# A linear-attention and MLP kernel: batch 2 loaded through POOL's queue, g spread by a DMA, and the first columns of w_in loaded in row pieces

## The chip, the cores and the metric

The kernel runs on one core of a Trainium2 chip. The core has a matrix engine (TensorE, called PE in the profile; its weight loads are the row PEld), a vector engine (VectorE, DVE), an activation engine (ScalarE, ACT), a general engine (GpSimd, POOL) and a queue engine that only issues transfers (SyncE, SP). Each engine takes its instructions in order. Transfers are issued from SP, ACT or POOL; SP and ACT hand them to hardware queues (q1 and q10 in the profile), POOL to the software queue (q0), which can also change the type on the way (float32 in memory to float16 on the chip). Matmuls write to PSUM, which has eight banks; VectorE and ScalarE read results from there.

The metric is the device time of one execution in microseconds, the median of several runs.

## The reference

Eight batches, eight heads, 576 rows, 64 columns per head. All inputs and the output are float32.

```python
kv  = einsum('bhsd,bhse->bhde', k, v)          # per head: k^T v, 64 x 64
out = einsum('bhsd,bhde->bhse', q, kv)
rms = sqrt(mean(out * out, axis=-1) + 1e-6)
x   = out / rms * g_norm                       # per head, then heads side by side: 4608 x 512
h   = x @ w_in                                 # 512 x 2048
y   = (h * sigmoid(1.702 * h)) @ w_out         # 2048 x 512
```

## The kernel before

**Tiling.** The MLP runs in nine steps, t = 0 to 8. Step t below 8 takes 512 of the 576 rows of batch t; the last step takes the 8 x 64 rows that are left over (`x_rem`). Within a step the hidden part makes 16 columns of 128 (`fo`), each by four matmuls (`ko`, line 457) into one PSUM bank, and ScalarE applies the gate (line 466) to float16 in `gT`. Then the output part makes four blocks of 128 rows (`mo`), each by 16 matmuls (line 492), and VectorE or ScalarE copies a block from PSUM (line 502); step 0 goes over its blocks in turns of four matmuls (`deep`), its first two blocks in pool ps_h, its last two in ps_o. The output is stored from SP (line 549 for steps 0 and 1, in eight pieces).

**Attention** of batch t + 1 is woven into step t by lists of due places: `at1(i, ...)` puts a call behind column i of the hidden part, `at2(i, ...)` behind matmul i of the output part. No planner decides anything: instructions go to each engine in the order in which the program writes them.

Batches 0 and 1 are loaded by POOL's queue straight to float16, 96 rows to a partition group (`early_load`, line 90); only batch 0's first pair of heads comes by SP and ACT. Batches 2 to 7 are loaded as float32 by SP (`load_batch`, lines 109 to 128): whole tiles `kf`, `vf`, `qf` of 1 MB, and the 64 rows left over, `krf`, `vrf`, `qrf`, in rows of 256 bytes. `casts(b)` then makes float16 of them, the tiles on VectorE and the rows on POOL (lines 130 to 143), `transpose_q` transposes q by DMA from SP, `kv` makes the 64 x 64 products (lines 220 to 235, with the left-over rows in a last matmul, line 233), `rows` and `turn` make the normalised rows, and a DMA transpose brings them to `xT`.

**Batch 2's load** is issued in step 0's output part. Its first tile is first written by a one-element POOL copy that reads the last tile of batch 1 (line 115), so that SP starts it when batch 1 has landed.

**The start.** Batch 0 goes pair by pair (two heads each; class `First`): `q(c)` transposes, `kv(c)` multiplies, `out(c)` makes q times kv, ScalarE squares, `sums(c)` adds up by a matmul with ones and takes the logarithm, `rs(c)` is the exponential, and `apply(c)` on VectorE (line 353) writes row block c of `xT`. Row block c is what the four-matmul sum of every hidden column needs at ko = c. The order of all this and of the first six columns (`GROUP`) is written out by hand, lines 579 to 627, with `busy(n)`, n matmuls whose result nobody reads, in between. POOL's queue holds, in order: pairs 1 to 3 of batch 0, w_in in five pieces (lines 181 to 185), w_out in four pieces and batch 1.

**PSUM.** ps_a (tag "att") has three banks, ps_h ("hT") three, ps_o ("o") two. A tile gets a bank that was released; a bank is released when the last reader of its tile in program order is done.

**g.** `g_col` (g along partitions, for `apply`) comes from two tiny matmuls (line 590). `g_all` (g along the free dimension on all partitions, for `turn`) comes from a matmul with a row of ones and a VectorE copy (`spread_g`, lines 636 to 639), behind column 9 of step 0.

Of the kernel before, what the change touches and what calls it, by code (L numbers as in the profile page):

```python
# [16 lines left out]
def kernel(  # L17
# [60 lines left out]
    ones_r = const.tile([1, P], F32)  # L78
# [30 lines left out]
    def load_batch(b, landed=None):  # L109
        tiles = {}  # L110
        for n in "kvq":
            t = tiles[n] = stage.tile([P, H, J * D], F32, name=f"{n}f", tag=f"{n}f")
            if landed is not None and n == "k":

                nc.gpsimd.tensor_copy(t[0:1, 0, 0:1], landed)
            nc.sync.dma_start(  # L116
                out=t, in_=srcs[n][b, :, 0:SM, :].rearrange("h (p j) d -> p h (j d)", j=J)
            )
        for n in "kv":
            t = tiles[n + "r"] = stage.tile([R, H, D], F32, name=f"{n}rf", tag=f"{n}rf")  # L120
            nc.sync.dma_start(out=t, in_=srcs[n][b, :, SM:S, :].rearrange("h p d -> p h d"))
        t = tiles["qr"] = stage.tile([P, 4, D], F32, name="qrf", tag="qrf")
        for g in range(2):
            nc.sync.dma_start(
                out=t[g * R : (g + 1) * R],
                in_=q[b, 4 * g : 4 * g + 4, SM:S, :].rearrange("h p d -> p h d"),
            )
# [53 lines left out]
    load_w_in(0, 4, 0, 2)  # L181
    load_w_in(0, 4, 2, KO)
    load_w_in(4, GROUP)
    load_w_in(GROUP, 10)
    load_w_in(10, FO)
# [8 lines left out]
    nc.vector.memset(ones_r, 1.0)  # L194
# [171 lines left out]
    class First(Attention):  # L366
# [4 lines left out]
        def kv(self, c):  # L371
            t = ps_o.tile([P, D], F32, name="kv0", tag="o")
# [16 lines left out]
        def q(self, c):  # L389
            t = ps_h.tile([P, S], F16, name="q0", tag="hT")  # L390
# [77 lines left out]
    def dense(t, units1, units2, group, deep, hid=None):  # L468
        hid = hid or Hidden(t)
        gT = hid.gT  # L470
        if group and t:
            for ko in range(KO):
                for fo in range(group):
                    hid.mm(ko, fo, *((ps_h, "hT") if fo < 3 else (ps_a, "att")))
# [106 lines left out]
    busy(2)  # L581
    a0.kv(0)
    busy(2)
    a0.out(0)
    a0.q(1)
    a0.kv(1)
    g_ps = ps_o.tile([P, 1], F32, name="g_ps", tag="o")
    for hl in range(2):
        r = slice(hl * D, (hl + 1) * D)
        nc.tensor.matmul(g_ps[r, :], g_row, one_t, start=True, stop=True)  # L590
    nc.vector.tensor_copy(g_col, g_ps)
    a0.sums(0)
    a0.out(1)
    a0.q(2)
    a0.rs(0)
    busy(1)
    a0.kv(2)
    a0.sums(1)
    a0.apply(0)
    busy(1)  # L600
    a0.out(2)
    a0.rs(1)
    a0.q(3)
    a0.kv(3)
    a0.sums(2)
    a0.apply(1)
    a0.out(3)
    a0.rs(2)
    a0.apply(2)
    busy(3)  # L610
    d0 = Hidden(0)
    for fo in range(4):
        d0.mm(0, fo, *((ps_h, "hT") if fo < 3 else (ps_a, "att")))
        if fo == 2:
            a0.ss(3)
# [115 lines left out]
```

## Time and profile before

| | us |
|---|---|
| median of five runs | 290.12 |
| lowest and highest | 288.58 and 290.89 |
| the profiled execution, its time | 289.17 |
| its span, first to last instruction | 287.1 |
| PE busy in it | 280.4 |
| ACT, DVE, POOL busy | 156.4, 110.9, 43.6 |
| granted TensorE clock | 1.0 throughout |

The profile shows one execution. A row of an engine's instructions in order of time gives the start in us from the beginning of the span, the time taken, the engine, the line of the kernel, the operation, the result and operands by the program's names, the shapes, how many instructions were merged (x29), and in brackets how long the engine was idle before and what ended that. A matmul's time runs from its start to its modelled end, and the next one starts before that, so the times of a row of matmuls overlap.

### The profile page before, as it was taken

What the parts mean: (1) busy time and instruction counts of PE and PEld (TensorE: products, weight loads), DVE (VectorE), ACT (ScalarE), POOL (GpSimd) and SP (SyncE); (2) the same over time, 40 slices, a digit from 0 to 9 for tenths busy, and PEclk for the clock granted to TensorE, in tenths of its full rate; (3) what the DMA queues carried; (4) which work ended last, traced back from release to release, by engine and by line L of the source; (5) the groups of instructions that cost most, each with busy time, mean ns of one, the idle gap of its engine ahead of it and who ended that gap; (6) DMA issues with size and microseconds to landing.
All of it is one profiled execution on the core that took longest, in us unless ns stands there. A gap on an engine that the chain in (4) does not pass through costs nothing.

```text
span 287.1 us, 4102 instructions
## 1 busy us (share of the span) xinstructions
PE 280.4 (98%) x1611; PEld 136.5 (48%) x1611; DVE 110.9 (39%) x221; ACT 156.4 (54%) x273; POOL 43.6 (15%) x59
## 2 busy tenths in 40 slices
PE   7899999999999999999999999999999999999994
PEld 2444544454445544554455445544554444444443
DVE  2530534437651566148603861376227400110011
ACT  2696457856565745584467536763666365017400
POOL 8941000301300140015000510032001100000000
PEclk9999999999999999999999999999999999999999
DMA  8999999979989736892879558953601130011022
GB/s 174 204 204 205 205 203 342 221 179 355 204 174 322 171 73 202 250 270 56 184 176 346 80 164 202 345 86 110 158 0 37 37 148 0 0 73 75 0 73 73
DMA packets 67300, 45.79 MB, mean 160 GB/s; under 512 B 37714, under 2 KB 65106, under 8 KB 66514
## 3 DMA queue, kind: packets, MB, share of 16 engines
q1 hardware_dynamic: 58064, 37.28, 50.0%
q0 software_dynamic: 8496, 7.29, 15.9%
q10 hardware_dynamic: 722, 0.97, 1.2%
q8 instruction: 12, 0.20, 0.3%
q14 instruction: 6, 0.05, 0.1%
HBM read 36.70 MB, written 9.44 MB: 161 GB/s over the span
## 4 chain that ended last, share of the span: by engine, by line
PE 84%; DMA 8%; POOL 2%; DVE 2%; SPq 2%; ACT 1%; issue 0%; POOLq 0%
PE hT L457 40%; PE o L492 37%; DMA krf<-in_k_dram 3%; DMA vbuf<-in_v_dram 2%; PE kvp L225 2%; PE outR L291 2%; DMA xT<-x 1%; PE oh L522 1%; SPq L116 1%; DMA out_dram<-osb 1%; POOL qraw L90 1%; ACT gT L466 1%; DVE kbuf L138 1%; PE ss L339 1%; POOL kraw L90 1%; PE outT L259 1%
## 5 line engine op out<-in xcount | busy, mean ns | idle before, releaser
L492 PE MATMUL o<-w_out_sb,gT 128*128 128x512 f16 x560 | 130.7, 379 | 0.0
L466 ACT ACTIVATE gT<-hT 128x512 f16<-128x512 f32 x144 | 84.8, 598 | 77.6 <-PE hT L457 77.5
L457 PE MATMUL hT<-xT,w_in_sb 128*128 128x512 f16 x512 | 116.4, 379 | 0.3 <-DMA xT<-x 0.3
L457 PEld LDWEIGHTS <-w_in_sb 128*128 128x128 f16 x576 | 55.1, 98 | 62.7 <-DMA xT<-x 0.8
L492 PEld LDWEIGHTS <-gT 128*128 128x128 f16 x560 | 53.0, 98 | 56.3 <-issue 0.2
L502 DVE COPY osb<-o 128x512 f32<-128x512 f32 x20 | 13.8, 691 | 63.5 <-PE o L492 63.5
L323 POOL TENSOR_TENSOR x<-xr,g_all 128x512 f16<-128x512 f32 x12 | 15.2, 1268 | 141.6 <-DVE xr L316 119.0
L240 DVE CAST kvb<-kvp 64x256 f16<-64x256 f32 (+1 forms) x16 | 6.2, 388 | 42.7 <-PE kvp L233 41.6
L302 DVE TENSOR_REDUCE sum<-sq 128x8 f32<-128x512 f16 x24 | 15.8, 678 | 17.5 <-ACT sq L299 17.5
L316 DVE TENSOR_TENSOR xr<-outR,sum 128x512 f32<-128x512 f32 x24 | 15.5, 686 | 11.1 <-ACT sum L313 11.1
L323 DVE TENSOR_TENSOR x<-xr,g_all 128x512 f16<-128x512 f32 x12 | 15.2, 1264 | 0.7
L299 ACT ACTIVATE sq<-outR 128x512 f16<-128x512 f32 x24 | 13.6, 591 | 2.0 <-PE outR L291 1.6
L279 ACT ACTIVATE sq<-outT 128x512 f16<-128x512 f32 (+1 forms) x16 | 7.7, 482 | 11.7 <-PE outT L259 10.4
L457 PE MATMUL hT<-x_rem,w_in_sb 128*128 128x512 f16 x64 | 14.0, 379 | 0.0
L502 ACT COPY osb<-o 128x512 f32<-128x512 f32 x15 | 8.7, 580 | 6.3 <-PE o L492 6.3
L312 ACT ACTIVATE sum<-sum,eps_t 128x16 f32<-128x16 f32 x12 | 3.7, 308 | 15.0 <-DVE sum L302 14.9
L341 ACT ACTIVATE ln<-ss,eps_t 128x512 f32<-128x512 f32 (+1 forms) x16 | 9.4, 585 | 3.2 <-PE ss L339 3.1
L138 DVE CAST qbuf<-qf 128x512 f16<-128x512 f32 x24 | 9.0, 436 | 3.8 <-DMA qf<-in_q_dram 3.8
L466 ACT ACT_TABLE_LOAD x8 | 10.3, 1283 | 0.1
L225 PEld LDWEIGHTS <-kbuf 128*128 128x128 f16 x96 | 7.4, 98 | 5.7
L291 PEld LDWEIGHTS <-qTd 128*128 128x128 f16 x96 | 7.4, 98 | 5.7 <-issue 0.2
L225 PE MATMUL kvp<-vbuf,kbuf 128*128 128x128 f16 x96 | 9.3, 219 | 0.0
(71 smaller groups left out, 152.6 us busy)
## 6 DMA issues: line engine op xcount, KB each, us to landing
kf<-in_k_dram SPq DMA_DIRECT2D x6, 1024.0 KB, 5.8
vf<-in_v_dram SPq DMA_DIRECT2D x6, 1024.0 KB, 8.4
qf<-in_q_dram SPq DMA_DIRECT2D x6, 1024.0 KB, 11.0
out_dram<-osb SPq DMA_DIRECT2D x6, 1024.0 KB, 4.3
w_out_sb<-in_moe_w_out_dram POOLq DMA_DIRECT2D x4, 512.0 KB, 16.8
out_dram<-osb SPq DMA_DIRECT2D x6, 192.0 KB, 3.2
out_dram<-osb SPq DMA_DIRECT2D x7, 128.0 KB, 2.4
w_in_sb<-in_moe_w_in_dram POOLq DMA_DIRECT2D x3, 256.0 KB, 6.7
```

The costliest lines, as they stand in the source:

```text
L138: nc.vector.tensor_copy(out=dst[:, c, :, :].rearrange("p j (l d) -> p j l d", l=2), in_=src[n][:, h, :].rearrange("p l (j d) -> p j l d", ...
L225: nc.tensor.matmul(t[:, c, :].rearrange("p (l d) -> p l d", l=2), kh[:, c, j, :], vh[:, 2 * c : 2 * c + 2, j * D : (j + 1) * D], start=(j ...
L291: nc.tensor.matmul(t[:, c * P : (c + 1) * P], self.qT[c][:, j * P : (j + 1) * P], self.kb[:, c, :], start=True, stop=True,)
L299: nc.scalar.activation(sq, t, AFT.Square)
L302: nc.vector.tensor_reduce(out=self.sum2[:, j % 2, :], in_=sq.rearrange("p (h d) -> p h d", h=H), op=ALU.add, axis=mybir.AxisListType.X,)
L316: nc.vector.tensor_mul(xr[:, i], self.o[j + i].rearrange("p (h d) -> p h d", h=H), s2[:, i, :].unsqueeze(2).to_broadcast([P, H, D]),)
L323: (nc.vector if i else nc.gpsimd).tensor_mul(self.x16[:, j + i, :].rearrange("p (h d) -> p h d", h=H), xr[:, i], g_all.unsqueeze(1).to_bro ...
L341: nc.scalar.activation(ln[:, 0:n], t[:, 0:n], AFT.Ln, bias=eps_t, scale=1.0 / D)
L457: nc.tensor.matmul(self.h[fo], w_in_sb[:, ko, fo * P : (fo + 1) * P], self.x[:, ko], start=(ko == 0), stop=(ko == KO - 1),)
L466: nc.scalar.activation(self.gT[:, fo, :], self.h[fo], AFT.Gelu_apprx_sigmoid)
L492: nc.tensor.matmul(os[mo], gT[:, fo, mo * P : (mo + 1) * P], w_out_sb[:, fo, :], start=(fo == 0), stop=(fo == FO - 1),)
L502: copy(osb[:, mo, :], os[mo])
```

## The change

Six edits:

- `load_batch` takes a queue, and loads q first, then the left-over rows of q, then k, v and their rows. Batch 2 is loaded by POOL's queue, issued behind the last of w_out and batch 1; the one-element copy that made SP wait is gone. Batches 3 to 7 stay on SP, in the new order.
- `g_all` is loaded by a DMA that repeats g over 128 partitions, on POOL's queue behind batch 2; `spread_g` and its row of ones are gone.
- w_in goes in seven pieces: row block 0 of columns 0 to 3 ahead of batch 0's last pair, then row block 1, row block 2 of these columns, row blocks 0 to 2 of columns 4 and 5, row block 3 of columns 0 to 5, and columns 6 to 7, 8 to 10 and 11 to 15 whole.
- The start's order is rewritten: first matmuls on w_in stand ahead of pair 3's transposes, and all six columns get their ko = 3 matmul last. Fillers go from 21 to 19. Pair 3 uses other PSUM pools. `g_col` is made earlier.
- Step 1 begins with a group of five columns instead of four; its first eight matmuls are as before, then the fifth column's first two, and the fifth column stands in ps_o.
- In step 1, the casts of batch 2, its transposes and the load of batch 3 stand behind column 5 instead of 7, and its kv products begin behind column 10 instead of 11.

```diff
--- before.py
+++ after.py
@@ -75,7 +75,6 @@
     eps_t = const.tile([P, 1], F32)
     g_col = const.tile([P, 1], F32)
     g_all = const.tile([P, D], F32)
-    ones_r = const.tile([1, P], F32)
     w_in_sb = const.tile([P, KO, DFF], F16)
     w_out_sb = const.tile([P, FO, DM], F16)
     x_rem = const.tile([P, KO, B * R], F16)
@@ -106,25 +105,23 @@
     qh = qbuf[:, 0 : NPAIR * SM].rearrange("p (c j e) -> p c j e", c=NPAIR, j=J)
     vh = vbuf.rearrange("p c x -> p (c x)")[:, 0 : NPAIR * SM].rearrange("p (h x) -> p h x", h=H)
 
-    def load_batch(b, landed=None):
+    def load_batch(b, queue=nc.sync):
         tiles = {}
-        for n in "kvq":
+        for n in "qkv":
             t = tiles[n] = stage.tile([P, H, J * D], F32, name=f"{n}f", tag=f"{n}f")
-            if landed is not None and n == "k":
-
-                nc.gpsimd.tensor_copy(t[0:1, 0, 0:1], landed)
-            nc.sync.dma_start(
+            queue.dma_start(
                 out=t, in_=srcs[n][b, :, 0:SM, :].rearrange("h (p j) d -> p h (j d)", j=J)
             )
+            if n == "q":
+                t = tiles["qr"] = stage.tile([P, 4, D], F32, name="qrf", tag="qrf")
+                for g in range(2):
+                    queue.dma_start(
+                        out=t[g * R : (g + 1) * R],
+                        in_=q[b, 4 * g : 4 * g + 4, SM:S, :].rearrange("h p d -> p h d"),
+                    )
         for n in "kv":
             t = tiles[n + "r"] = stage.tile([R, H, D], F32, name=f"{n}rf", tag=f"{n}rf")
-            nc.sync.dma_start(out=t, in_=srcs[n][b, :, SM:S, :].rearrange("h p d -> p h d"))
-        t = tiles["qr"] = stage.tile([P, 4, D], F32, name="qrf", tag="qrf")
-        for g in range(2):
-            nc.sync.dma_start(
-                out=t[g * R : (g + 1) * R],
-                in_=q[b, 4 * g : 4 * g + 4, SM:S, :].rearrange("h p d -> p h d"),
-            )
+            queue.dma_start(out=t, in_=srcs[n][b, :, SM:S, :].rearrange("h p d -> p h d"))
         staged[b] = tiles
 
     def casts(b):
@@ -178,11 +175,15 @@
     for c in range(1, NPAIR):
         for n in "qkv"[c == 1 :]:
             early_load(n, 0, c, c + 1)
-    load_w_in(0, 4, 0, 2)
-    load_w_in(0, 4, 2, KO)
-    load_w_in(4, GROUP)
-    load_w_in(GROUP, 10)
-    load_w_in(10, FO)
+        if c == NPAIR - 2:
+            load_w_in(0, 4, 0, 1)
+    load_w_in(0, 4, 1, 2)
+    load_w_in(0, 4, 2, 3)
+    load_w_in(4, GROUP, 0, 3)
+    load_w_in(0, GROUP, 3, KO)
+    load_w_in(GROUP, 8)
+    load_w_in(8, 11)
+    load_w_in(11, FO)
 
     nc.scalar.preload_act_table_set("natural_log_exp_and_others")
     nc.vector.memset(ones2, 0.0)
@@ -191,7 +192,6 @@
     nc.vector.memset(eps_t, EPS)
     one_t = const.tile([1, 1], F32)
     nc.vector.memset(one_t, 1.0)
-    nc.vector.memset(ones_r, 1.0)
 
 
     def load_w_out(f0, f1):
@@ -369,7 +369,8 @@
         ss_pool = (ps_o, "o")
 
         def kv(self, c):
-            t = ps_o.tile([P, D], F32, name="kv0", tag="o")
+            pool, tag = (ps_o, "o") if c < NPAIR - 1 else (ps_a, "att")
+            t = pool.tile([P, D], F32, name="kv0", tag=tag)
             for j in range(NJ):
                 for hl in range(2):
                     x = slice((hl * NJ + j) * D, (hl * NJ + j + 1) * D)
@@ -387,7 +388,8 @@
             )
 
         def q(self, c):
-            t = ps_h.tile([P, S], F16, name="q0", tag="hT")
+            pool, tag = (ps_h, "hT") if c < NPAIR - 1 else (ps_o, "o")
+            t = pool.tile([P, S], F16, name="q0", tag=tag)
             for j in range(NJ):
                 for hl in range(2):
                     nc.tensor.transpose(
@@ -469,9 +471,11 @@
         hid = hid or Hidden(t)
         gT = hid.gT
         if group and t:
-            for ko in range(KO):
-                for fo in range(group):
-                    hid.mm(ko, fo, *((ps_h, "hT") if fo < 3 else (ps_a, "att")))
+            order = [(ko, fo) for part in (range(4), range(4, group)) for ko in (0, 1) for fo in part]
+            order += [(ko, fo) for ko in range(2, KO) for fo in range(group)]
+            for ko, fo in order:
+                pool = (ps_h, "hT") if fo < 3 else (ps_a, "att") if fo == 3 else (ps_o, "o")
+                hid.mm(ko, fo, *pool)
             for fo in range(group):
                 hid.gate(fo)
         for fo in range(FO):
@@ -578,51 +582,55 @@
 
     busy(12)
     a0.q(0)
-    busy(2)
     a0.kv(0)
-    busy(2)
-    a0.out(0)
-    a0.q(1)
-    a0.kv(1)
     g_ps = ps_o.tile([P, 1], F32, name="g_ps", tag="o")
     for hl in range(2):
         r = slice(hl * D, (hl + 1) * D)
         nc.tensor.matmul(g_ps[r, :], g_row, one_t, start=True, stop=True)
+    busy(2)
+    a0.out(0)
     nc.vector.tensor_copy(g_col, g_ps)
+    a0.q(1)
+    a0.kv(1)
     a0.sums(0)
     a0.out(1)
+    busy(1)
     a0.q(2)
     a0.rs(0)
+    a0.sums(1)
     busy(1)
     a0.kv(2)
-    a0.sums(1)
     a0.apply(0)
+    a0.rs(1)
+    busy(2)
+    a0.out(2)
     busy(1)
-    a0.out(2)
-    a0.rs(1)
-    a0.q(3)
-    a0.kv(3)
+    d0 = Hidden(0)
+    d0.mm(0, 0)
+    d0.mm(0, 1)
+    d0.mm(0, 2)
     a0.sums(2)
     a0.apply(1)
+    a0.q(3)
+    a0.rs(2)
+    a0.kv(3)
+    d0.mm(1, 0)
+    d0.mm(1, 1)
     a0.out(3)
-    a0.rs(2)
+    d0.mm(1, 2)
+    d0.mm(0, 3, ps_a, "att")
+    d0.mm(1, 3)
     a0.apply(2)
-    busy(3)
-    d0 = Hidden(0)
-    for fo in range(4):
-        d0.mm(0, fo, *((ps_h, "hT") if fo < 3 else (ps_a, "att")))
-        if fo == 2:
-            a0.ss(3)
-            a0.apply(3)
-    for ko in (1, 2):
-        for fo in range(4):
-            d0.mm(ko, fo)
-    for ko in range(KO - 1):
-        d0.mm(ko, 4, ps_o, "o")
-    for fo in range(GROUP - 1):
+    d0.mm(2, 0)
+    a0.ss(3)
+    a0.apply(3)
+    for fo in range(1, 4):
+        d0.mm(2, fo)
+    for fo in range(4, GROUP):
+        for ko in range(3):
+            d0.mm(ko, fo, ps_o, "o")
+    for fo in range(GROUP):
         d0.mm(KO - 1, fo)
-    for ko in range(KO):
-        d0.mm(ko, GROUP - 1, ps_o, "o")
     for fo in range(GROUP):
         d0.gate(fo)
     load_w_out(0, 4)
@@ -632,11 +640,9 @@
         early_load("k", 1, c, c + 2)
         early_load("v", 1, c, c + 2)
         load_w_out(8 + 2 * c, 12 + 2 * c)
-
-    def spread_g():
-        t = ps_a.tile([P, D], F32, name="ga_ps", tag="att")
-        nc.tensor.matmul(t, ones_r, g_row, start=True, stop=True)
-        nc.vector.tensor_copy(g_all, t)
+    load_batch(2, nc.gpsimd)
+
+    nc.gpsimd.dma_start(out=g_all, in_=g_norm.unsqueeze(0).to_broadcast([P, D]))
 
     live = {0: a0}
 
@@ -662,7 +668,6 @@
             at2(4, of(0, "ss", NPAIR, True))
             at2(4, of(0, "apply", NPAIR))
             at1(8, start, 1)
-            at1(9, spread_g)
             for r in krem + vrem:
                 at1(8, nc.vector.memset, r[R:P], 0.0)
             for c in range(NPAIR):
@@ -674,21 +679,20 @@
                 at2(o, of(1, "out", c))
                 at2(o + 7 - c // 2, of(1, "ss", c))
                 at2(o + 7 - c // 2, of(1, "apply", c))
-            at2(14, load_batch, 2, vbuf[0:1, NPAIR - 1, 0:1])
         elif b < B:
             if t == 1:
                 at2(46, setattr, live[1], "ss_pool", Attention.ss_pool)
                 at2(46, of(1, "out", NPAIR))
                 at2(53, of(1, "ss", NPAIR))
                 at2(53, of(1, "apply", NPAIR))
-            f0 = 7 if t == 1 else 2
+            f0 = 5 if t == 1 else 2
             at1(f0, casts, b)
             at1(f0, start, b)
             at1(f0, of(b, "transpose_q"))
             if t + 2 < B:
                 at1(f0, load_batch, t + 2)
             for c in range(NPAIR):
-                at1((11 if t == 1 else 9) + c, of(b, "kv", c))
+                at1((10 if t == 1 else 9) + c, of(b, "kv", c))
             at2(6, nc.scalar.preload_act_table_set, "natural_log_exp_and_others")
             for j in range(J):
                 at2((1, 4, 8, 11)[j], of(b, "rows", j))
@@ -697,7 +701,7 @@
             at2(27, of(b, "out", NPAIR))
             at2(36, of(b, "ss", NPAIR))
             at2(36, of(b, "apply", NPAIR))
-        dense(t, u1, u2, (GROUP, 4)[t] if t < 2 else 0, t == 0, None if t else d0)
+        dense(t, u1, u2, (GROUP, 5)[t] if t < 2 else 0, t == 0, None if t else d0)
 
 
 # ---- launch: one core; inputs and outputs as the reference has them ----
```

## The prediction

> **What bounds the kernel now.** I read the page first, then the chain in order of time, then each engine's instructions in order of time for 5 to 20 us and 38 to 80 us.
>
> ```profile
> PE 280.4 (98%) x1611; PEld 136.5 (48%) x1611; DVE 110.9 (39%) x221; ACT 156.4 (54%) x273; POOL 43.6 (15%) x59
> ```
>
> TensorE is the bound. A busy matmul is drawn 379 ns long, but the next starts 216 ns after it (24 of them between 23.95 and 28.92 us: 4.97 / 23), so "busy" hides small waits, and I look for them in start-to-start distances. After 13 us all excess over the usual distances comes to only 1.9 us. That caps what better order can bring there; the rest must come from the first 14 us, where filler matmuls run.
>
> ```profile
> 12.89 0.38 PE L376 MATMUL kv<-vbuf,kraw 96*64 96x64 f16 x12 [0.58 <-DMA vbuf<-in_v_dram]
> 13.20 0.39 PE L339 MATMUL ss<-sq,ones 128*128 128x512 f16 x1
> 13.66 0.39 PE L259 MATMUL outT<-qT,kvb 128*128 128x512 f16 x1
> 13.88 0.81 PE L571 MATMUL idle<-kvb 128*128 128x512 f16 x3
> 14.53 0.81 PE L457 MATMUL hT<-xT,w_in_sb 128*128 128x512 f16 x3
> 15.18 0.38 PE L339 MATMUL ss<-sq,ones 128*128 128x512 f16 x1
> 15.39 6.42 PE L457 MATMUL hT<-xT,w_in_sb 128*128 128x512 f16 x29
> ```
>
> Here the last pair's values land at 12.76, the first matmul on w_in starts at 14.53, and from 15.39 on there is no gap. The other tight places are t = 0 to 1, batch 2's arrival, and t = 1 to 2:
>
> ```profile
> 48.77 0.75 DVE L353 SCALAR_TENSOR_TENSOR xT<-outT,g_col,rs 128x512 f16<-128x512 f32 x1 [0.97 <-ACT rs L347]
> 49.44 0.68 DVE L502 COPY osb<-o 128x512 f32<-128x512 f32 x1
> ...
> 54.63 0.89 POOL L143 CAST krem<-krf 64x512 f16<-64x512 f32 x1 [14.80 <-DMA krf<-in_k_dram]
> 55.47 0.80 POOL L143 CAST vrem<-vrf 64x512 f16<-64x512 f32 x1
> ...
> 58.25 0.39 PE L225 MATMUL kvp<-vbuf,kbuf 128*128 128x128 f16 x4
> 58.47 0.22 PE L233 MATMUL kvp<-vrem,krem 128*128 128x128 f16 x1
> ...
> 78.40 3.84 PE L457 MATMUL hT<-xT,w_in_sb 128*128 128x512 f16 x17 [0.26 <-DMA xT<-x]
> ```
>
> The reader should see a VectorE copy (mo = 2 of t = 0) that ends at 50.12 behind an apply, batch 2's row casts that end at 56.27 for a matmul at 58.47, and the one wait TensorE has later. By start distance that wait is 0.42 (the last output matmul starts at 77.76, the next could at 77.98).
>
> **Part 1, pieces of w_in and order of the start.** POOL's queue moves 200 to 205 GB/s from 6 to 40 us and lands in order. A 128 KB row piece ahead of pair 3 is 0.64 us, so pair 3's values land at 13.40. The other pieces follow at about 14.0, 14.7, 15.8 and 16.8, each before its matmul below; the last ends near 23.5, and its first matmul (column 11) is due near 24.7. POOL issues three DMAs more for w_in; at 0.72 to 0.76 each they hide behind a queue that lags 5.5 us.
>
> I walked the new order through TensorE, VectorE and ScalarE with the rows of before: matmuls 0.216 apart, twelve transposes 0.30, twelve kv matmuls 0.31; qT copy 0.46, kvb 0.29, apply 0.75; square 0.60, Ln 0.68, Exp 0.63; 0.05 from a result to its user. The same walk over the old order gives 14.44 for the first w_in matmul (measured 14.53) and 28.74 for the last (28.92), so I trust it to 0.3. New order: apply(0) waits behind kvb(2) and ends at 12.65 (was 12.38); the first w_in matmul starts at 12.70, 1.8 earlier; ss(2) 13.35; q(3) 13.6; kv(3) 13.9 (was 12.89; now its place in the order, not the landing, holds it); out(3) 14.8 (13.66); x(2) is ready at 15.95, mm(2,0) waits 0.35 for it with ss(3) queued behind, ss(3) 16.2 (15.18), and apply(3) ends at 18.82 (17.73). By then TensorE has done 18 of the group's 24 matmuls and stands still for 0.45; the last six end the group at 20.2 (19.93). The first gate moves from 18.40 to 19.3, gate 6 ends at 22.9, and column 9 waits about 0.1 for its PSUM slot. So the filler removed (21 down to 19) and the 1.8 us head start are paid back by a chain that ends 1.1 later. Dropping g's spread returns 0.45 (from 23.28 + 0.22 to 23.95). Sum at the end of t = 0's hidden part: **+0.1**, bounds -0.5 to +0.6. Moving g_col's two matmuls up, and the pair-3 tiles to other PSUM slots, meets only slots long free in this walk.
>
> **Part 2, a group of five at t = 1.** The fifth column takes a slot of ps_o, and both are held by t = 0's last outputs. Slots go round in order of release (as at 47.83, where the third column waits 0.08 for the Ln that had the slot), so it gets that of mo = 2, whose copy ends at 50.12. The matmul is due at 47.62 + 0.08 + 8 x 0.216 = 49.43 and can start at 50.17: **+0.74**. The wait that goes is that of column 4 for the first gate: 48 matmuls from 47.62 span 10.79, of which 47 x 0.216 + 0.38 = 10.53 is work, 0.08 the Ln wait, so 0.20 is left: **-0.20**. If the fifth column gets the other slot (ScalarE's copy ends 49.21) only the -0.20 stays. Range -0.20 to +0.54; I take +0.54. The matmuls behind it in the order (x(2), x(3) of batch 1, ready by 49.52) wait with it; no data is then late.
>
> **Part 3, batch 2 on POOL's queue.** SP loses seven load issues (39.86 to 50.9) and POOL the wait for vbuf and a 0.18 cast; POOL gains seven issues and g's broadcast, some 6 us at the 0.8 of its 768-row load, in a stretch where it is idle (26.8 to 54.6). POOL's issues from 15.85 on each start when the eighth transfer before landed. By that q goes out near 29, the others before 40, and the queue goes on without a gap behind the last w_out piece, near 41.3. Order q, q rows, k, v, k rows, v rows: 3.54 MB at the 340 to 360 GB/s of 44 to 50 us, with the rows of 256 B slower as at 50 to 54 us (about 220), ends near 52.5 with nothing beside it. But SP is now free, and the eight output stores go out as their copies end (45.3, 47.5, 49.2, 50.1) and no longer at 51.0: 1 MB, some 2.7 us of the same transfer time at the rows' rates. So the v rows land near 56, and up to 2.5 later if the transpose of q, now at 52 and not 57.2, gets half the engines. SP's issue of that transpose is moved ahead; the casts on VectorE can start behind the 50.12 copy. TensorE asks for v rows one column earlier, but Part 2 holds it back: 47.7 + 44 x 0.216 + 0.08 + 0.74 gives 58.0 for kv(0), 58.2 for its row matmul. A cast of 0.7 to 0.8 must start by 57.5. Central case **0**, bounds 0 to +2.0 (landing at 58.7 with a 0.8 cast gives 1.3; a slow 256 B rate on this queue the rest). g's broadcast lands after that, and its first user was at 67.8: 0.
>
> The Trainium skill, DMA: Bandwidth & Descriptors, section "Issuing engines are not separate DMA queues", says that all issuing engines feed the same 16 DMA engines and only issue time is saved. By it alone the move would bring 0 and the earlier stores would simply take from the load. The rows of before show no transfers of POOL and SP side by side for long enough to weigh it. SBUF — State Buffer, section "SBUF: two separate sides", warns that VectorE copies in a fast mode lock POOL out of writing descriptors; by it the four copies at 28.71 (1.16 us) would delay an issue by up to 1.16, hidden by 10 us of queue.
>
> **Part 4, later.** Load of batch 3 waits in SP for q's second transpose, and that for POOL's third cast: near 59.5 against 61.38. Its tail shared the engines with the x transposes that landed at 78.35 (4.26 us against 3.1 in the median). With TensorE 0.64 later and the load 1.9 earlier, the 0.42 wait goes: **-0.42**, bounds -0.42 to 0. From batch 3 on the new order q, rows, k, v changes nothing that TensorE waited for: 0, as loads run a batch ahead.
>
> Sum: 0.1 + 0.54 + 0 - 0.42 = **+0.2 us**. The profiled execution took 289.17 (span 287.1 and 2.1 around it), 0.95 under the median of 290.12, within the runs' 288.58 to 290.89; so 289.4 on its own scale, 290.3 on the median's.
>
> **Rivals.**
> (a) Slower, by one mechanism: batch 2's v rows land after 57.5 and TensorE stands at the row matmul of kv(0), each us of lateness one us. It decides (over 0.5%) past about 58.7. For it: stores and transposes now overlap the load; against: v rows came at 54.6 before with as many bytes. Time 291.6 (stall 1.3) to 292.3 (stall 2.0).
> (b) Faster: no slot wait (-0.74), the start at its low bound (-0.6): 289.0, or 288.7 with the median's luck. For it: 1.8 us head start; against: the chain to apply(3).
> (c) The change does not do what it says: the early piece moves only idle time, pair 3's delay costs nothing; that is my case within 0.3.
> (d) The start's gaps (about 0.5 us at 6.6, 10.3, 18.4) cool the clock: the first twelve fillers were 0.43 apart and not 0.216. A stretch of 3 to 4 us at that pace costs 1.5 to 2. Against: gaps of 0.3 to 0.6 at 6.0, 9.1 and 12.3 before, after which matmuls stayed at 0.216.
>
> **Numbers.** About 0.5% (1.45 us) is what a measurement here can tell from no change. Chances: my case with small variants (and (c)) 0.62, (a) 0.24, (d) 0.04, (b) past the bound 0.10. Hence faster 0.10, same 0.62, slower 0.28. Range 289.0 (all low bounds: -0.5 - 0.20 - 0.42) to 292.6 (a stall of 2 and about half of the other high bounds, 0.6 and 0.54).
>
> **What would show it.** First w_in matmul near 12.7 and apply(3) ending near 18.8; a gap of 0.7 in the first matmuls of t = 1 that ends with the VectorE copy; output stores issued from 45 us; POOL's v-row cast ending before TensorE's row matmul near 58.2; no wait near 78. Wrong if the v rows land past 58, if the fifth column finds a free slot, or if TensorE starts the gates before 19.

## The result, and the profile after

| | before | after |
|---|---|---|
| median, us | 290.28 | 288.82 |
| lowest and highest | 288.58 and 291.13 | 288.43 and 289.89 |
| executions | 52 | 28 |
| the profiled execution, its time | 289.17 | 289.13 |
| its span | 287.1 | 287.0 |

The ratio is 0.996, with a 95% interval of 0.9949 to 0.9971, where +0.2 us was forecast. By the ratio that is 1.2 us faster and by the medians 1.46; the times before lean to the upper side, and the ratio stands nearer to the means (290.06 and 288.89). 288.82 lies 0.18 below the forecast's range. The spread is part of the result. Of the times before, half lie between 289.55 and 290.54; of those after, half lie between 288.61 and 289.01. Both kernels can come to 288.6; 6 of the 52 executions before and 21 of the 28 after took at most 289.01. A few executions on record, both traced ones of the kernel "all but the start" (below) among them, ran at a granted clock of 0.56 to 0.76 and took 371 to 497 us; no median or ratio here counts them.

The two profiled executions cannot be subtracted to find the gain: they took 289.17 and 289.13. The one before was 1.1 quicker than its median, the one after 0.3 slower than its own. What they can show is where a wait stands. A wait is read here from the distance between the starts of two neighbouring matmuls, less the 0.216 that is usual ("by start distance"); the idle time in brackets is shorter, since it counts from a matmul's modelled end.

TensorE's row of the page after stands beside 280.4 us and 1611 matmuls before:

```profile
PE 280.4 (98%) x1607; PEld 135.9 (47%) x1607; DVE 110.8 (39%) x219; ACT 156.2 (54%) x273; POOL 51.0 (18%) x69
```

Four matmuls fewer (two fillers and the two passes of g's spread), and no less busy. The start after, TensorE's instructions in order of time (start, time taken, engine and line, as in the prediction):

```profile
13.08 0.81 PE L459 MATMUL hT<-xT,w_in_sb 128*128 128x512 f16 x3
13.72 0.38 PE L339 MATMUL ss<-sq,ones 128*128 128x512 f16 x1
14.03 0.45 PE L395 MATMUL q<-ident,qraw 96*64 96x96 f16 x12
14.31 0.35 PE L377 MATMUL kv<-vbuf,kraw 96*64 96x64 f16 x12
14.62 0.60 PE L459 MATMUL hT<-xT,w_in_sb 128*128 128x512 f16 x2
15.23 0.39 PE L259 MATMUL outT<-qT,kvb 128*128 128x512 f16 x1
15.46 1.24 PE L459 MATMUL hT<-xT,w_in_sb 128*128 128x512 f16 x4
16.54 0.38 PE L339 MATMUL ss<-sq,ones 128*128 128x512 f16 x1
16.75 2.10 PE L459 MATMUL hT<-xT,w_in_sb 128*128 128x512 f16 x9
19.14 1.67 PE L459 MATMUL hT<-xT,w_in_sb 128*128 128x512 f16 x7 [0.28 <-DVE xT L353]
```

The first matmul on w_in comes 1.45 earlier than before (13.08 against 14.53), and the last pair's products 1.42 later (14.31 against 12.89). At 19.14 TensorE has no work left that does not need the last `apply`, and waits for it, as the prediction said of the chain. From there on:

```profile
35.91 0.49 PE L424 MATMUL kvp<-vbuf,kbuf 96*128 96x128 f16 x6 [0.19 <-DMA vbuf<-in_v_dram]
...
48.06 9.73 PE L459 MATMUL hT<-xT,w_in_sb 128*128 128x512 f16 x44
57.62 0.39 PE L225 MATMUL kvp<-vbuf,kbuf 128*128 128x128 f16 x4
57.85 0.22 PE L233 MATMUL kvp<-vrem,krem 128*128 128x128 f16 x1
...
78.21 4.05 PE L459 MATMUL hT<-xT,w_in_sb 128*128 128x512 f16 x18
```

Three things are to be seen. At 35.91 the products of batch 1 wait for its values (0.35 by start distance), which they did not before (they started at 35.47). The 44 matmuls of step 1 run from 48.06 without a gap; the stall of 0.74 that the prediction put among them is not there. The matmuls of step 2 start at 78.21 with no bracket: the wait for `xT` before step 2 is gone.

The marks along TensorE, in us (starts, from the traces; "step 1 long" is the distance of the two starts, before rounding):

| | last `apply` ends | first w_in matmul | step 1 | batch 2's kv | step 2 | step 1 long | step 2 to last matmul |
|---|---|---|---|---|---|---|---|
| before | 17.73 | 14.53 | 47.62 | 58.25 | 78.40 | 30.79 | 204.64 |
| after | 19.08 | 13.08 | 48.05 | 57.62 | 78.21 | 30.16 | 204.83 |

So in these two executions the start costs 0.44, step 1 gives back 0.63, and 0.19 goes again behind step 2 (one start distance at 138.0 is 0.21 too long). The bracket names nothing there, but the landings do: the second x transpose for step 4 lands at 138.07, and the matmul due at 138.00 starts at 138.21. In all seven traces with batch 2 on POOL's queue step 4 starts within 0.14 of that landing and is 0.07 to 0.25 late; in the five with batch 2 on SP the transpose had landed some 0.5 before. So the change pays a little there. That is 0.0 in sum, and the gain of the medians is not in it.

What moved on SP, VectorE and POOL. SP's issues after:

```profile
45.74 6.59 SPq L553 DMA_DIRECT2D out_dram<-osb  x8
53.04 3.92 SPq L244 DMA_TRANSPOSE qTd<-qbuf  x1
57.37 1.17 SPq L246 DMA_TRANSPOSE qTr<-qrem  x1
58.59 0.58 SPq L112 DMA_DIRECT2D qf<-in_q_dram  x1
```

Before, SP's row was:

```profile
39.86 0.41 SPq L116 DMA_DIRECT2D kf<-in_k_dram  x1
...
48.28 2.62 SPq L124 DMA_DIRECT2D qrf<-in_q_dram  x2
51.01 6.09 SPq L549 DMA_DIRECT2D out_dram<-osb  x8
57.20 2.84 SPq L244 DMA_TRANSPOSE qTd<-qbuf  x1
...
61.38 0.58 SPq L116 DMA_DIRECT2D kf<-in_k_dram  x1
```

The stores began at 51.01, the transpose of q at 57.20 and batch 3's load at 61.38: all of SP's work is 2.8 to 5.3 us earlier after the change. The casts of the left-over rows after, on POOL:

```profile
55.33 0.73 POOL L140 CAST krem<-krf 64x512 f16<-64x512 f32 x1 [11.26 <-DMA krf<-in_k_dram]
56.02 0.80 POOL L140 CAST vrem<-vrf 64x512 f16<-64x512 f32 x1
```

The cast of the v rows ends at 56.82, and TensorE asks for them at 57.85.

### The profile page after: what moved, and what is told of

Same layout as the page of the kernel before. It is cut to its first block, busy times and chain, and to the rows that moved or that the text cites. A ratio compares the mean times of both kernels' runs of the same rounds, so it can differ in the third digit from the quotient of the medians.

```text
span 287.0 us, 4100 instructions
## 1 busy us (share of the span) xinstructions
PE 280.4 (98%) x1607; PEld 135.9 (47%) x1607; DVE 110.8 (39%) x219; ACT 156.2 (54%) x273; POOL 51.0 (18%) x69
## 4 chain that ended last, share of the span: by engine, by line
PE 86%; DMA 11%; POOL 1%; issue 1%; DVE 0%; POOLq 0%
PE o L496 40%; PE hT L459 39%; DMA vbuf<-in_v_dram 6%; DMA w_in_sb<-in_moe_w_in_dram 2%; DMA qraw<-in_q_dram 2%; PE kvp L225 2%; PE outR L291 2%; PE oh L526 1%; POOL w_in_sb L168 1%; PE ss L339 1%; PE kvp L424 1%; PE kvp L233 0%; PE outT L259 0%; PE outT L270 0%; POOL kraw L89 0%
## 5 line engine op out<-in xcount | busy, mean ns | idle before, releaser
L302 DVE TENSOR_REDUCE sum<-sq 128x8 f32<-128x512 f16 x24 | 15.8, 679 | 18.3 <-ACT sq L299 18.3
L133 DVE CAST vbuf<-vf 128x512 f16<-128x512 f32 x24 | 9.4, 453 | 1.6 <-DMA vf<-in_v_dram 1.6
```

Source lines behind the costliest of these rows:

```text
L133: nc.vector.tensor_copy(out=vh[:, h, :], in_=src["v"][:, h, :])
L302: nc.vector.tensor_reduce(out=self.sum2[:, j % 2, :], in_=sq.rearrange("p (h d) -> p h d", h=H), op=ALU.add, axis=mybir.AxisListType.X,)
```

## The experiments

Two theories stood at the start. T takes the traces at their word: the load of batch 2 on POOL's queue brings the gain, by waits that go in step 1 and at step 2, and the start costs. S: the start brings it, in executions whose traces were not kept, and the load brings little. A third, C, is about the start alone: its loss comes from the order of the chain of pairs, and not from the piece of w_in ahead of pair 3.

### The kernel before, twice more

Both are unchanged copies, each profiled once.

> The kernel before, unchanged, profiled once more: its 52 times lie in two groups, 15 at 288.6 to 289.6 and 37 at 289.7 to 291.1, and the profile read so far (289.17) is of the lower one. Theory T (the transfers of batch 2 and 3): an execution of the upper group differs from 78 us on, where the first matmuls of step 2 wait for the x transposes; that wait, 0.42 us in the profile read, is 1.5 to 2.5 us, and everything before it stands within 0.3. Rival S (the start): the upper group has its first matmul on w_in 1 to 1.5 us later than 14.53 (pair 3 landing late, or the slow clock of the first fillers lasting longer), and the wait at 78 stays below 0.5. If this execution is of the lower group, neither shows.

> The same once more, for a second chance at an execution of the upper group (70 of 100 by the times). T: wait at 78 us of 1.5 to 2.5 us if the execution takes over 290. S: first w_in matmul near 15.5 to 16 if it takes over 290.

Measured: 289.56 and 289.58, again under the median of the timed executions beside them (290.31). The wait at step 2 was 0.66 by start distance in the first, and in the second 0.47, with another 0.41 at batch 2's products, where the trace of before had none. TensorE in the second:

```profile
58.58 0.38 PE L225 MATMUL kvp<-vbuf,kbuf 128*128 128x128 f16 x4 [0.25 <-DVE vbuf L136]
...
78.78 4.49 PE L457 MATMUL hT<-xT,w_in_sb 128*128 128x512 f16 x20 [0.31 <-DMA xT<-x]
```

What follows: the late waits of the kernel before (those at batch 2's products and at step 2) are no constant. They summed to 0.43, 0.66 and 0.88 in three executions, all of them on the quick side. The 0.42 of one trace was the smallest sample of something that varies.

### The start alone

The kernel before with the seven pieces of w_in, the rewritten order and the PSUM pools of pair 3.

```diff
-    load_w_in(0, 4, 0, 2)
-    load_w_in(0, 4, 2, KO)
...
+        if c == NPAIR - 2:
+            load_w_in(0, 4, 0, 1)
+    load_w_in(0, 4, 1, 2)
+    load_w_in(0, 4, 2, 3)
+    load_w_in(4, GROUP, 0, 3)
+    load_w_in(0, GROUP, 3, KO)
...
+    d0.mm(0, 2)
...
+    a0.q(3)
```

> Before with the start alone changed: w_in's row pieces, the hand-written order, the PSUM pools of pair 3. Batch 2 on SP, group of four, g by matmul as before. T: the same as before within 0.3 us, with the same two groups of times (median 290.1 to 290.6). S: the gain is here, median 288.8 to 289.2 and a narrow spread. By the prediction's walk the end of step 0's hidden part moves by +0.5 (without g's spread removed).

Measured: 291.42 (290.0 to 291.99), ratio 1.0041 (1.0022 to 1.006). That is 1.1 slower by the medians and 1.2 by the ratio, which is neither theory's number. Its TensorE at three places:

```profile
14.64 0.38 PE L381 MATMUL kv<-vbuf,kraw 96*64 96x64 f16 x12 [0.68 <-DMA vbuf<-in_v_dram]
...
59.73 0.38 PE L229 MATMUL kvp<-vbuf,kbuf 128*128 128x128 f16 x4 [0.40 <-DVE vbuf L136]
...
80.16 3.20 PE L463 MATMUL hT<-xT,w_in_sb 128*128 128x512 f16 x14 [0.54 <-DMA xT<-x]
```

Here the last pair's values do end a wait (0.68). Step 1 starts at 48.55, 0.93 later than before, and both late waits are there, 0.56 and 0.70 by start distance. What follows: S falls. The start is a loss, and with batch 2 on SP the late waits stay; in this trace they are longer than in the three of the kernel before.

### The load alone

The kernel before with batch 2 on POOL's queue, the new order of loads, and the places behind column 5 and column 10. Start, group of four and g's matmul are those of before.

```diff
-    def load_batch(b, landed=None):
+    def load_batch(b, queue=nc.sync):
...
-        for n in "kvq":
+        for n in "qkv":
...
+    load_batch(2, nc.gpsimd)
...
-            at2(14, load_batch, 2, vbuf[0:1, NPAIR - 1, 0:1])
...
-            f0 = 7 if t == 1 else 2
+            f0 = 5 if t == 1 else 2
...
-                at1((11 if t == 1 else 9) + c, of(b, "kv", c))
+                at1((10 if t == 1 else 9) + c, of(b, "kv", c))
```

> Before with the load part alone changed: batch 2 by POOL's queue, order q, k, v, casts and load of batch 3 behind column 5, kv behind column 10. Start, group of four and g by matmul as before. T: the whole gain is here, median 288.6 to 289.2, spread narrow, no wait at 78. S: median 290 to 290.6 with two groups as before. If kv of batch 2 stands still for its v rows (one column earlier without the longer group), a gap of up to 1 us at 57 to 58 us.

Measured: 289.15 (288.88 to 289.38 in 12 executions), ratio 0.9973 (0.9961 to 0.9984): 1.16 faster by the medians, 0.8 by the ratio. No start distance near 57 or 78 is too long. The times also draw together here: 0.5 from lowest to highest, against 1.6 of the kernel before beside it (289.12 to 290.69). T holds in its direction; by the ratio it is two thirds of the gain, not the whole.

### All but the start

The kernel after with the start of before, run twice.

```diff
-        if c == NPAIR - 2:
-            load_w_in(0, 4, 0, 1)
...
+    load_w_in(0, 4, 0, 2)
+    load_w_in(0, 4, 2, KO)
...
+            t = ps_o.tile([P, D], F32, name="kv0", tag="o")
```

> After with the old start put back (old order, old five pieces of w_in, old PSUM pools of pair 3); load of batch 2, group of five and g by DMA as in after. By the sum of the traces (the start costs +0.95 in front_alone up to step 1, g's spread gives 0.45, group of five 0.20, the load the rest): 288.1 to 288.5, so 0.4 to 0.7 faster than after and 1.8 to 2.2 faster than before. If the start and the load need each other, it is not faster than after (288.8).

> After with the old start put back, once more, beside after on the same chip, and for a readable profile. 288.3 to 288.6; 0.3 to 0.5 faster than after. Its profile: apply(3) ends near 17.7, step 1 starts near 47.1 (47.6 less 0.45), no wait at 57 and 78.

Measured: 288.40, ratio 0.9945 (0.9929 to 0.996), and 288.66, ratio 0.9941 (0.9927 to 0.9954), with times of 288.06 to 288.8. Neither left a trace that can be compared with the others, so where this kernel still waits is not seen.

What follows: the rest of the change is worth about 1.6 to 1.9 by the medians (1.6 to 1.7 by the ratio), and the start takes back 0.3 to 0.4 of it. The changed kernel beside the second run stands at 0.9956 (below), and their intervals overlap: the sign rests on the start alone, which cost 1.1, and on the marks (step 1 at 47.59 in the kernel under "g by its matmul", which has the old start and even keeps g's matmul, against 48.05), the size of 0.3 on the medians.

### The changed kernel once more

An unchanged copy, beside the one above.

> The changed kernel unchanged, beside late_again: 288.8 to 289.1.

Measured: 288.96 (288.65 to 289.76), ratio 0.9956 (0.994 to 0.9971). Its last `apply` ends at 19.42, 0.34 later than in the first trace of the same kernel, because a matmul at 16.64 waited 0.56 for a piece of w_in. Yet batch 1's products start at 35.90 in it and at 35.91 in the other: the one with the quicker start waits there for batch 1's first values, which land at 35.78 in it (34.15 in the kernel before), and the other, which comes 0.34 later, finds them landed at 35.62. What is won on the way to 30 us is given back at 36.

### The early piece behind pair 3

```diff
-        if c == NPAIR - 2:
-            load_w_in(0, 4, 0, 1)
+    load_w_in(0, 4, 0, 1)
     load_w_in(0, 4, 1, 2)
```

> After with the first row piece of w_in moved back behind pair 3; the order by hand and the other pieces as in after. Theory C (the start is paced by the chain through the order by hand, x(2) to ss(3) to x(3)): within 0.3 us of after, apply(3) still ends near 19.1. Rival L (it is paced by pair 3's landing, which the piece and the wait of POOL's ninth load for its first put off): kv(3) starts 0.5 to 1 us earlier, apply(3) ends near 18.3 and the time falls by 0.4 to 0.8.

Measured: 289.18 (288.96 to 289.37), ratio 0.9972 (0.9958 to 0.9987), about 0.3 above the changed kernel. Its TensorE and the last `apply` on VectorE:

```profile
13.37 0.82 PE L458 MATMUL hT<-xT,w_in_sb 128*128 128x512 f16 x3 [0.82 <-DMA w_in_sb<-in_moe_w_in_dram]
```

```profile
18.64 0.75 DVE L352 SCALAR_TENSOR_TENSOR xT<-outT,g_col,rs 128x512 f16<-128x512 f32 x1 [2.06 <-ACT rs L346]
```

Pair 3's values land at 12.70 here, well ahead of its products (14.61), so rival L, that pair 3's landing alone makes the chain late, falls. But now the first three w_in matmuls wait for their weights, the chain behind them with them, and the last `apply` ends at 19.38, as late as with the piece ahead. With the piece ahead a landing holds the chain too in three of the traces: pair 3's values land at 13.80 to 14.59, and its products are 0.10, 0.23 and 0.68 late for them (the 0.68 is in the start alone); in the first trace of the changed kernel they land at 13.90 for products at 14.31, and the order alone holds them. What follows: given the written order, with pair 3's products behind the first w_in matmuls, moving the early piece does not help; it trades one wait for another. That the order by itself would make the chain this late is favoured, not shown: no run has this order without such a wait and compares it.

### A group of four in step 1

```diff
-        dense(t, u1, u2, (GROUP, 5)[t] if t < 2 else 0, t == 0, None if t else d0)
+        dense(t, u1, u2, (GROUP, 4)[t] if t < 2 else 0, t == 0, None if t else d0)
```

The order of the matmuls in the group is that of before too.

> After with step 1's group of four again. The prediction's slot wait would make it 0.54 faster than after. By the trace of after, where the fifth column waits for ScalarE's copy and starts without a gap, it is 0.20 slower: the wait of the next column for the first gate is back.

Measured: 289.00 (288.45 to 290.16), ratio 0.9966 (0.9951 to 0.9982). In its trace the wait for the first gate is back, 0.20 at 51.35, and step 1 is 30.36 long instead of 30.16. The trace gives 0.20 and the medians 0.2, though the intervals overlap: the fifth column saves its 0.20, and no cost of it is seen.

### The order of loads alone, on SP

The kernel before with q and its rows first in `load_batch`; batch 2 stays on SP.

```diff
-        for n in "kvq":
+        for n in "qkv":
```

> Before with only the order of a batch's loads changed to q, q rows, k, v, k rows, v rows; batch 2 still on SP behind its wait, old due places. Theory O (the order does it, because the casts of q on VectorE no longer wait for the last of three tiles): median 288.9 to 289.5, no wait at 57 or 78. Theory Q (the queue does it: SP blocked by its load issues sends stores and transposes late): 289.9 to 290.5, the wait at 78 stays above 0.3, stores still issued from 50 us on.

Measured: 289.56 (289.1 to 290.47), ratio 0.9988 (0.9973 to 1.0003): between the ranges of the two theories, and open whether it gains at all. The casts of q start at 50.28 instead of 53.96, but SP and step 2 stay:

```profile
50.59 6.05 SPq L550 DMA_DIRECT2D out_dram<-osb  x8
```

```profile
78.69 4.49 PE L458 MATMUL hT<-xT,w_in_sb 128*128 128x512 f16 x20 [0.31 <-DMA xT<-x]
```

The stores wait behind SP's load issues as before, and the wait for `xT` is still there (0.47 by start distance). A wait at batch 2's products is not, and the median is 0.75 below that of the kernel before, twice what the ratio says. So the order may bring a part of the gain; that it does is neither shown nor excluded.

### The queue of batch 2 alone

The kernel before with one thing changed: batch 2 goes by POOL's queue, in the old order k, v, q, rows, and everything in step 1 keeps its old place. (The rows go last in the kernel that ran, not ahead of q.)

```diff
-    def load_batch(b, landed=None):
+    def load_batch(b, queue=nc.sync):
...
-            nc.sync.dma_start(
+            queue.dma_start(
...
+    load_batch(2, nc.gpsimd)
...
-            at2(14, load_batch, 2, vbuf[0:1, NPAIR - 1, 0:1])
```

> Before with only batch 2's queue changed: on POOL, in the old order k, v, k rows, v rows, q last, old due places. Theory Q (the queue frees SP, so that stores, transposes and batch 3's load go earlier): no wait at 78, but q lands last, so that the casts on VectorE start only near 53 and kv of batch 2 may wait at 57 to 58 by up to 1 us; median 289.1 to 289.8. Theory O (the order alone matters): 290 to 290.5, waits as before.

Measured: 288.96 (288.67 to 289.05), ratio 0.995 (0.9937 to 0.9964), a little below what theory Q expected. Its SP and its TensorE:

```profile
45.56 6.74 SPq L546 DMA_DIRECT2D out_dram<-osb  x8
55.10 1.93 SPq L241 DMA_TRANSPOSE qTd<-qbuf  x1
```

```profile
58.50 0.39 PE L222 MATMUL kvp<-vbuf,kbuf 128*128 128x128 f16 x4
...
78.23 5.13 PE L454 MATMUL hT<-xT,w_in_sb 128*128 128x512 f16 x23
```

What follows: the queue alone suffices for the gain of the load part: 1.30 by the medians and 1.45 by the ratio, against 1.16 and 0.8 with the order and the places (the two intervals just overlap). Both late waits are gone, with q's casts and transposes still behind column 7. What it shares with the load alone, and what the order on SP lacks, is the freed SP: stores from 45.6 and not from 51, and the transpose of q and batch 3's load 2.1 and 2.5 us earlier.

How this reaches step 2 can be followed in the landings. The x transposes of batch 2 go out from SP behind batch 3's load, at 70 to 74. Before, that load lands only at 75.2, and the first transpose, issued at 71.06, takes 6.6 us and lands at 77.64, the second at 78.36. With the order alone it is the same (issued at 70.03, landed at 77.94, then 78.65). With the queue alone the load has landed by 73.1; the transposes, issued at 70.04 and 74.36, take 3.8 and 3.1 us and land at 73.83 and 77.43, ahead of the matmul due near 78.

The Trainium skill, "DMA: Bandwidth & Descriptors", section "Issuing engines are not separate DMA queues", says that issuing from several engines saves only the issue time, which is usually small beside the transfer itself. The measurement agrees with the cause and not with the size. In the kernel before, SP's seven issues for batch 2 took from 39.86 to 50.9, and eight stores whose data was ready from 45.3 on stood in line behind them.

### g by its matmul

All but the start, with g spread by the matmul and the VectorE copy of before.

```diff
-    nc.gpsimd.dma_start(out=g_all, in_=g_norm.unsqueeze(0).to_broadcast([P, D]))
...
+    def spread_g():
+        t = ps_a.tile([P, D], F32, name="ga_ps", tag="att")
+        nc.tensor.matmul(t, ones_r, g_row, start=True, stop=True)
+        nc.vector.tensor_copy(g_all, t)
...
+            at1(9, spread_g)
```

> late_again with g spread by the matmul and copy as before. By the distance of 0.45 from the last matmul of column 9 to the first of column 10 beyond the usual one: 0.4 to 0.5 slower than late_again, and nothing at the turn of batch 2 (its first user of g is past 67). If the DMA of g cost something in the queue, less.

Measured: 288.74 (288.58 to 288.98), ratio 0.9946 (0.9932 to 0.996), 0.08 above the same kernel with the DMA beside it (0.15 by the ratios). The 0.45 of TensorE time that g's matmul takes at 23.3 is not worth 0.45 in the median. Why is open: the kernel with the DMA left no trace to compare, and in this one batch 1's first values land at 34.94 for products at 35.45, which would leave room for nearly all of it.

### Where it adds up

In us, each against the kernel before or its neighbour run beside it:

| part | by the medians | by the ratios |
|---|---|---|
| batch 2 on POOL's queue, alone | -1.30 | -1.45 |
| the same with order and places | -1.16 | -0.8 |
| group of five | about -0.2 | about -0.2 |
| g by DMA | -0.08, open why not more | -0.15 |
| the start | +1.1 alone, about +0.3 with the rest | +1.2 alone, about +0.4 with the rest |
| sum, with the start at +0.3 | -1.1 to -1.3 | -0.7 to -1.4, with +0.4 |
| measured | -1.3 to -1.46 | -1.16 to -1.28 |
| measured, all but the start | -1.6 to -1.9 | -1.6 to -1.7 |

The best version is the change without its start, 288.40 and 288.66 in two runs. It beats the kernel before clearly, and the changed one by some 0.3, with overlapping intervals.

What stays open: the traces of the kernel before show 0.43 to 0.88 of late waits, and taking them away brings 1.2 to 1.3 in the medians (0.8 to 1.45 by the ratios). All three of them are of executions at 289.6 or less, so nothing shows where the slower half of this kernel loses the remaining 0.5. That the same waits are longer there is argued. Two things point to it: they differ from trace to trace, and in the one kept trace of a slower execution with batch 2 on SP, that of the start alone (290.93, 1.76 above the first trace of before), they make up the difference: 0.93 is a later step 1, and 0.83 are longer late waits (1.26 against 0.43). From step 2 to the last matmul the five traces with batch 2 on SP agree within 0.03. The seven traces with batch 2 on POOL's queue have neither wait. The spread settles nothing: it is 0.5 with the load alone, but 1.5 for the changed kernel and 1.7 with the group of four.

## Why the prediction was wrong

**Two steps failed: the size of Part 4's -0.42, and the sign of Part 2's +0.54.** Of Part 4 the mechanism was right: batch 3's load starts 2.8 earlier and the wait at step 2 is gone. The size was read from one execution that lay 0.95 under the median, and was then also made the upper end of what could be gained ("bounds -0.42 to 0"). The same wait measured 0.47 and 0.66 in two other traces, with 0.41 more at batch 2's products. By the timed runs the load on POOL's queue is worth 1.2 to 1.3 by the medians, 0.8 to 1.45 by the ratios. The prediction named the 0.95 and only shifted its sum by it. It should have asked which waits can make an execution 0.95 longer; those on transfers are the first to suspect, and the change takes two of them away.

**Part 2's +0.54 should have been -0.20.** The prediction gave the fifth column the slot of mo = 2, freed by a VectorE copy. In the kernel after, the column's first matmul waits for ScalarE: it has the slot of mo = 3. The copies of step 0's last blocks, on ScalarE and on VectorE:

```profile
49.08 0.57 ACT L506 COPY osb<-o 128x512 f32<-128x512 f32 x1
```

```profile
49.87 0.68 DVE L506 COPY osb<-o 128x512 f32<-128x512 f32 x1
```

ScalarE's copy ends at 49.65, before the ninth matmul of step 1 is due (48.06 + 0.08 + 8 x 0.216 = 49.87); it starts on time, at 49.85, when VectorE's copy, which ends at 50.55, is not done. The prediction had this case as its lower end and chose the other, by a rule on the order of release taken from one other place.

**Part 1's +0.1 was too small, with the right mechanism.** At its own mark, the end of step 0's hidden part, the first output matmul starts at 29.24 and 29.57 in the two traces, against 29.14: +0.10 and +0.43. On the way there the last `apply` ended at 19.08 and 19.42 (18.82 was worked out), the first w_in matmul came at 13.08 and 12.50 (12.70), and the group of 24 matmuls ended at 20.43 and 20.77, 0.51 and 0.84 later than before (0.27 was worked out). g's spread gave back about 0.4 (0.45 was said). Mis-sized was the early piece: it took 1.09 and 1.35 us of POOL's queue and not 0.64, so that pair 3's values landed at 13.9 instead of 13.40, and w_in's row block 2 at 15.20 and 16.60 instead of 14.7, in the second trace 0.56 too late for its matmul. Then comes what the prediction did not look at. Batch 1's first values land at 35.78 instead of 34.15, and in the execution with the quicker start this costs 0.35. Step 1 starts 0.44 and 0.43 later, against 0.1. Why the values land later is not settled. Their issue moved from 15.85 to 18.21, since w_in's three pieces more stand ahead of it, but they land 18.3 us after it before and 17.6 after; the kernel before had them at 34.15, 34.61 and 34.27, and with the early piece behind pair 3, and as many pieces, they were there at 34.16. The prediction checked the pieces' own issues against the queue's lag, and not what stands behind them.

**Part 3's 0 was right.** The stores went out from 45.74 (45.3 was said), the v rows were cast by 56.82 for a matmul at 57.85. The prediction gave 54.6 for the v rows of before; that is the k rows (54.58), and the v rows landed at 55.35 before and at 55.85 after. Rival (a), the late v rows, had one us to spare; rival (d), a cooler clock, did not come: the changed kernel's executions were granted 0.997 to 1.0. Rival (b) came near in time, by half of its reason and for the rest by luck: no slot wait, but no gain at the start; the late waits made up what that lacked.

**The sum** by what was measured: start +0.3 to +0.4, group -0.2, the load -1.2 to -1.3 (-0.8 to -1.45 by the ratios). By the prediction: +0.1, +0.54, -0.42. Part 2 was 0.74 too slow and Part 4 some 0.8; Part 1, the other way, was 0.2 to 0.3 too fast.

## What to carry to other kernels

When the profiled execution is quicker than the median, ask which waits may be short in it by luck: here a change that removed 0.4 of waits on transfers in one trace was worth 0.8 to 1.45 in the timed runs. An engine that only issues transfers can be a bound of its own: read what stands behind its longest issues, and what has been ready since when. And before a saving is booked on the busiest engine, look for the next landing that it needs: here 0.35 of a quicker start was lost at one.

## What the runs showed of the hardware

**POOL's queue made larger packets of the same load.** Queues between 40 and 54 us, with packets, MB and share of the 16 engines, first after, then before:

```profile
q0 software_dynamic: 1310, 3.85, 94.0%
q1 hardware_dynamic: 309, 0.52, 11.9%
```

```profile
q1 hardware_dynamic: 4574, 3.64, 94.4%
q0 software_dynamic: 264, 0.25, 11.0%
```

That is 2.9 KB to a packet against 0.8 KB over all that moved, with the ends of earlier loads; batch 2's own packets are of 4,096 B on POOL's queue, and of 1,024 B and 256 B on SP's. The prediction had put the rows of 256 bytes on this queue at their rate on SP's (220 GB/s); in these 14 us the whole moved 4.38 MB after and 3.90 MB before.

**A VectorE copy grew beside an issue by POOL.** The four copies of batch 1's q, on VectorE, and the first issue for batch 2 beside them:

```profile
29.42 1.58 DVE L96 COPY qbuf<-qraw 96x768 f16<-96x768 f16 x4 [9.13 <-DMA qraw<-in_q_dram]
```

```profile
29.68 0.90 POOL L112 DMA_DIRECT2D qf<-in_q_dram  x1 [2.16 <-DMA qraw<-in_q_dram]
```

The four took 1.16 before; now the third of them took 776 ns and not 349, and 774 to 778 in all seven kernels with an issue of batch 2 on POOL beside it. The Trainium skill's page "SBUF — State Buffer", section "SBUF: two separate sides", which the prediction drew on, has such copies hold up POOL; it also says that whichever of the two starts first keeps the shared port, and the other waits. Here the issue took 0.90, against 0.89 and 0.88 for the two behind it in the kernel with the queue alone, and it was VectorE that took longer; that the port is the reason, no trace shows. The 0.4 lay beside other work.

**POOL's ninth issue waited for the first landing.** Before, the k values of pair 3 were the eighth transfer on this queue and went out at 6.40 without a wait. After, with the early piece ahead of them, they are the ninth, and their issue waits 0.38 for the landing of the first:

```profile
7.41 0.63 POOL L89 DMA_DIRECT2D kraw<-in_k_dram  x1 [0.38 <-DMA qraw<-in_q_dram]
```

The first and the ninth transfer signal their landing by the same one of eight semaphores, which the program uses in turn, so this is a wait of the program's; that the queue itself would hold the ninth is not shown. In the second trace of the changed kernel the first had landed at 6.67, and the ninth went out at 6.96 without a wait.
